# w2's block sums made by accumulating transfers, with the splits that follow them in a new order

## Chip, cores, metric

One core of one Trainium2 chip. The metric is the device time of one execution in microseconds (us). The engines are called PE (TensorE, matmuls), DVE (VectorE), ACT (ScalarE), POOL (GpSimd) and SP (SyncE, which issues DMA transfers). Each runs its own instructions in order and waits for the others by semaphores.

## What is computed

```python
xn = layernorm(x)                                 # x: 2048 x 576
q, k, v = split(xn @ wqkv)                        # 32 heads of 18
phi = lambda t: where(t > 0, t + 1, exp(t)) + 1e-6
kv = einsum("hsd,hse->hde", phi(k), v); z = phi(k).sum(over s)
s = ((phi(q) @ kv) / (phi(q) . z + 1e-6)) @ wo    # linear attention
h = gelu_tanh(xn @ w1 + b1)                       # 2048 x 4608
g = silu(h @ w2 + b2)                             # 2048 x 576
out = x + s * g
```

All is float32 at float32 precision.

## The kernel before

**Operands.** PE multiplies in a reduced form (fp32r). Each factor is therefore split in two: a rounded copy (hi, a cast on ACT) and the remainder (lo, a subtraction on DVE), and a product is hi x hi, hi x lo and lo x hi. Most products are also done by a two-by-two Strassen-Winograd scheme: seven products of block sums in place of eight of blocks. So the sums of a weight's blocks must be made and split before PE can use them.

**w2's blocks.** w2 has nine chunks of four row tiles. A chunk's blocks B(r, n) are two row tiles by half the columns (288). Four sums are needed of each: 5, 6, 4 and 7, by the numbers of the products that use them. POOL makes them with `tensor_tensor`: 5 and 6 of all chunks (and 4 of the first) early, beside the attention part, by `w2_sum`; `w2_hi` (ACT) and `w2_lo` (DVE, tile w2o) split them and SP stores them in HBM, from where the chunk steps load them. The sums 7 and 4 of the later chunks are made within the chunk steps by `sum7` and `sum4` (one and two instructions on POOL).

**The stages in time.**

- Keys: up to 163 us. Eight pairs of row tiles; a pair p has 14 steps (`at_step`). In them PE projects keys and values and sums the state kv; ACT and DVE normalise, transpose and split the next pairs' x, and do phi.
- Rounds of queries, 163 to about 283 us. A round r has 14 steps as well: PE projects two tiles of queries (products 1, 6, 7, 5, 2, 4, 3, tiles a, b, z, e) and multiplies the round before by the folded kw. POOL multiplies queries by z (`den_mul`) and divides them (`den_div`).
- Chunk steps, about 283 us to the end. Eighteen steps of 28 places each: nine chunks for one half of the rows, then nine for the other. A step makes h by two groups of seven products (`Up`), splits h and its sums, and adds seven down products (tile pm) into macc. In the first half it also makes the sums of w1 and w2 for the next chunk. The second half loads what the first has stored.

**The order** is written out by hand: `add(step, fn, ...)` puts a call in a list, `at_step` runs the list after the matmuls of that step, and `in_order` keeps every engine to the order of the calls. So an instruction that waits holds all later ones of its engine. SP's transfers are in such an order too.

**Names.** `wkq` is the weight of keys, later of queries; `split_sums(j)` splits its block sums. `xSL`, `xSH` are the splits of x's block sums. `split_kw(k)` splits row tile k of kw, after a transfer that shifts its rows (kr). `SUMS[j]` lists w2's early sums by (chunk, sum).

Of the kernel before, what the change touches and what calls it, by code (L numbers as in the profile page):

```python
# [8 lines left out]
F32 = mybir.dt.float32  # L9
# [6 lines left out]
P = 128  # L16
S = 2048
D = 576
# [8 lines left out]
CF = 4  # L27
# [15 lines left out]
def linear_attention_gated_ffn(ctx, tc, x, wqkv, wo, w1, b1, w2, b2, out):  # L43
# [97 lines left out]
    class Weight:  # L141
# [28 lines left out]
        def sums(self, raw, eng):  # L170
# [8 lines left out]
            for i, u, v in ((5, f1a, f0a), (6, f1b, T[5]), (7, f1b, f1a), (4, f0b, T[6])):  # L179
                eng.tensor_tensor(T[i], u, v, op=SUB)  # L180

        def split_sums(self, j, elo):
            self.put(lambda t: t[:, 3 + 2 * j : 5 + 2 * j], self.t[j], elo)

# [130 lines left out]
    def s_lo(p):  # L315
        cs = pair_cols(p)
        nc.vector.tensor_tensor(
            xSL[:, :, cs], s_raw[:, :8], xSH[:, :8, cs].bitcast(F32), op=SUB
        )
        r = xSH[64:, 8, cs]  # L320
        nc.vector.tensor_tensor(r, s_raw[64:, 8], r.bitcast(F32), op=SUB)

# [142 lines left out]
    w2raw, w2op = {}, {}  # L465

    def w2_load(c, pool, tag):
        src = w2[c].rearrange("p (a r n d) -> p a r n d", a=2, r=2, n=2)
        if tag == "wa":
            tiles = [pool.tile([P, KT * 2 * P], F32, tag=tag, name=f"w2r{c}{r}") for r in range(2)]  # L470
            parts = [t[:, : 2 * D].rearrange("p (a n d) -> p a n d", a=2, n=2) for t in tiles]
            for r in range(2):
                nc.sync.dma_start(parts[r], src[:, :, r])
        else:
            t = pool.tile([P, CF * D], F32, tag=tag, name=f"w2r{c}")
            nc.sync.dma_start(t, w2[c])
            t = t.rearrange("p (a r n d) -> p a r n d", a=2, r=2, n=2)
            parts = [t[:, :, r] for r in range(2)]
        w2raw[c] = parts

    def w2_block(c, i):

        B = lambda r, n: w2raw[c][r][:, :, n, :]
        return {
            5: (B(0, 0), B(0, 1), B(0, 0)),
            6: (B(1, 1), B(1, 1), B(0, 0)), 4: (B(1, 0), B(1, 0), B(1, 1)),
        }[i]

    def w2_sum(j):
        c, i = SUMS[j]  # L490
        dst, a, b = w2_block(c, i)
        nc.gpsimd.tensor_tensor(dst, a, b, op=SUB)

    def w2_hi(j):
        w2op[j] = w1r.tile([P, 2, 2, HD], F32R, tag="stw", name=f"w2o{j}")
        nc.scalar.copy(w2op[j][:, 0], w2_block(*SUMS[j])[0])

    def w2_lo(j):
        c, i = SUMS[j]
        t = w2op.pop(j)  # L500
        nc.vector.tensor_tensor(t[:, 1], w2_block(c, i)[0], t[:, 0].bitcast(F32), op=SUB)  # L501
        w2_dram[c, i] = d = dram.tile([P, 2, 2, HD], F32, name=f"op_{c}_{i}")
        nc.sync.dma_start(d, t.bitcast(F32))
# [93 lines left out]
    K_UP = (1, 6, 7, 5, 2, 4, 3)  # L597
    W2_FIRST = {2: (0,), 3: (1, 2), 4: (3,), 5: (4, 5), 6: (6,)}

    def plan_pair(p):  # L600
# [19 lines left out]
        if p == 1:  # L620
# [21 lines left out]
            add(base + 6, load_x, 4, 1)  # L642
            add(base + 6, wkq.split_sums, 0, DV)
        else:
# [27 lines left out]
        add(base + 8, phi_max, kb, eb)  # L672
        add(base + (11 if p == 1 else 10), phi_add, kb)
        add(base + 12, k_sum, kb)
        for n, j in enumerate(W2_FIRST.get(p, ())):
            add(base + (1, 3)[n], w2_sum, j)
            add(base + (4, 9)[n], w2_hi, j)
            add(base + (6, 12)[n], w2_lo, j)
        if p in (1, 3):
            add(base + 13, w2_load, {1: 1, 3: 2}[p], w2p, "w2r")  # L680
        if p == 4:
# [3 lines left out]
        if p == 7:  # L685
            add(base, nc.gpsimd.memset, kvz, 0.0)
            add(base + 5, lambda: wkq.split_sums(1, DV))
            add(base + 5, lambda: wkq.split_raw(cur["rq"][0], 0, DV))
            add(base + 9, lambda: wkq.split_sums(0, DV))
            add(base + 10, lambda: wkq.split_rest(cur["rq"][1], DV))  # L690
            add(base + 11, lambda: wkq.split_raw(cur["rq"][0], 1, DV))
        if p == 6:
            add(base + 9, lambda: wkq.sums(cur["rq"][0], GP))

# [51 lines left out]
    def load_w2_raw(n):  # L746
        raw = w2rp.tile([P, CF // 2, 2, 2, HD], F32, tag="w2raw", name=f"w2raw{n}")
        nc.sync.dma_start(raw.rearrange("p a b n d -> p (a b n d)"), w2[n % NC])
        return raw
# [222 lines left out]
    for r in range(NPAIR + 2):  # L972
# [186 lines left out]
    class W2:  # L1159
# [5 lines left out]
        def load_raw(self):  # L1165
            self.raw = raw = load_w2_raw(self.n) if self.n else w2_raw0[0]
            self.B = lambda r, n: raw[:, :, r, n, :]
            self.src = {1: self.B(0, 0), 2: self.B(1, 0), 3: self.B(1, 1), 7: self.B(0, 1)}

        def sum7(self):  # L1170
            nc.gpsimd.tensor_tensor(self.src[7], self.src[3], self.src[7], op=SUB)

        def sum4(self):
            tt = nc.gpsimd.tensor_tensor
            self.src[4] = self.src[2]
            tt(self.src[4], self.src[2], self.src[7], op=SUB)
            tt(self.src[4], self.src[4], self.src[1], op=SUB)

        def plain(self, f):
            self.src["p", f] = self.raw[:, f // 2, f % 2]  # L1180

# [14 lines left out]
    class HOps:  # L1196
# [11 lines left out]
        def S(self, i, pr):  # L1208
            A = lambda r, c: self.A[pr, r, c]
            tt = nc.gpsimd.tensor_tensor  # L1210
            src = self.src
            if i == 5:
                src[5, pr] = A(1, 0)
                tt(src[5, pr], A(1, 0), A(1, 1), op=ADD)  # L1214
            elif i == 6:
                src[6, pr] = A(0, 0)
                tt(src[6, pr], src[5, pr], A(0, 0), op=SUB)  # L1217
            elif i == 3:
                src[3, pr] = A(0, 1)
                tt(src[3, pr], A(0, 1), src[6, pr], op=SUB)  # L1220
# [21 lines left out]
    DST = {1: U1, 2: C11, 5: C22, 3: C12, 6: U1, 7: C22, 4: C21}  # L1242
    BIAS = {2: 0, 7: 1, 3: 1, 4: 0}

    def product(c, i, q2, hs, w, held):

        wh, wl = w
        ps = held.pop((CHAIN[i], q2)) if i in CHAIN else bank2(f"pm{i}")
        if i in CHAIN.values():
            held[i, q2] = ps  # L1250
        for q in range(2):
            cs = slice((q2 + q) * P, (q2 + q + 1) * P)
            seq = [(st, m, p) for p in range(2) for st, m in ((0, wh), (0, wl), (1, wh))]
            for n, (st, m, p) in enumerate(seq):
                nc.tensor.matmul(  # L1255
                    ps[:, q, :HD], hs[p][st][:, cs], m[:, p, :],
                    start=(n == 0 and i not in CHAIN), stop=(n == len(seq) - 1),
                    skip_group_check=True,
                )
        src, dst = ps[:, :, :HD], macc[:, q2 : q2 + 2, DST[i], :]  # L1260
        if c > 0 or i in (5, 6):
            nc.vector.tensor_tensor(dst, src, dst, op=ADD)  # L1262
        elif i in BIAS:
            h = BIAS[i]
            bb = b2b[:, None, h * HD : (h + 1) * HD].to_broadcast([P, 2, HD])
            nc.vector.tensor_tensor(dst, src, bb, op=ADD)
        else:
            nc.vector.tensor_copy(dst, src)

    def combine(s, eng, q=slice(0, QH)):  # L1270
        A = lambda s: macc[:, q, s, :]
        eng.tensor_tensor(A(s), A(s), A(U1), op=ADD)

# [146 lines left out]
    PW2 = {1: 3, 7: 4, 3: 6}  # L1420
    PW2_FIRST = {1: 3, 7: 4, 2: 5, 3: 6}
    W2_SUMS_NEXT = {5: 23, 6: 27}
# [22 lines left out]
    for step in range(n_chunks):  # L1445
# [15 lines left out]
        if half == 0 and c < NC - 1:  # L1461
# [116 lines left out]
```

## Time and profile before

| what | value |
|---|---|
| runs (us) | 1120.46, 1120.64, 1121.62; median 1120.64 |
| profiled execution | 1120.46 us, its span 1118.8 us |
| PE, DVE, ACT, POOL busy (us) | 1099.8, 834.3, 506.2, 485.2 |
| DMA | 257.16 MB, 230 GB/s in the mean, 64.3% of 16 engines' span |
| granted PE clock | 1.00 over the span |

Times in a row of the profile are microseconds from the span's start. A row of the timeline gives start, duration, engine, line, operation and tiles (out<-in), and in brackets the idle time before it with what ended it. Busy time of PE is modelled, since matmuls overlap; how far apart two matmuls start tells more than how long each is.

### The profile page before, as it was taken

To read this page: it belongs to the slowest core of one execution; us is meant where nothing else is said; L and a number is where in the kernel's file an instruction comes from. 1 tells how busy PE (TensorE), PEld (TensorE's weight loads), DVE (VectorE), ACT (ScalarE), POOL (GpSimd) and SP (SyncE) were. 2 spreads that over 40 slices of the span, in tenths; PEclk is the share of its full clock that TensorE was granted. 3 is DMA by queue.
4 is the path that set the end of the run, shared out by engine and by line. 5 is a ranking of instruction groups with operands and counts; after the bars stand their busy time and mean duration, and the time that the engine had idled before them with its cause. 6 is when DMAs were issued, how large, how long until landed. Compare 5 with 4: busy or idle time off the path is not lost.

```text
span 1118.8 us, 18673 instructions
## 1 busy us (share of the span) xinstructions
PE 1099.8 (98%) x6924; PEld 1014.6 (91%) x6924; DVE 834.3 (75%) x1250; ACT 506.2 (45%) x913; POOL 485.2 (43%) x411
## 2 busy tenths in 40 slices
PE   8999999999999999999999999999999999999997
PEld 7899998999898998989989889899898998988987
DVE  6878756777598988989889888666475574664756
ACT  6766554445545454454454544524233242242352
POOL 5654434655364645645556443324224133242340
PEclk9999999999999999999999999999999999999999
DMA  5855537774968468385583759977666666666243
GB/s 202 289 210 224 223 99 238 279 281 161 354 253 322 179 234 296 153 326 193 207 323 149 294 181 369 373 261 267 217 207 215 211 200 210 228 200 222 88 136 119
DMA packets 89098, 257.16 MB, mean 230 GB/s; under 512 B 9581, under 2 KB 20333, under 8 KB 86959
## 3 DMA queue, kind: packets, MB, share of 16 engines
q1 hardware_dynamic: 89007, 255.96, 64.3%
q8 instruction: 55, 0.90, 0.3%
q14 instruction: 36, 0.29, 0.1%
HBM read 155.03 MB, written 100.01 MB: 228 GB/s over the span
## 4 chain that ended last, share of the span: by engine, by line
PE 82%; DVE 7%; ACT 4%; issue 2%; DMA 2%; POOL 2%; SPq 0%; DVEq 0%; POOLq 0%; ACTq 0%
PE pm L1255 32%; PE e L1118 12%; PE zy L1118 10%; PE a L1118 10%; PE b L1118 4%; PE pl L404 4%; PE ps_s L866 2%; PE pd L1372 2%; PE e L349 1%; DVE w2o L501 1%; DMA kr<-kw 1%; DVE h_l L896 1%; PE z L349 1%; PE ps_kva L457 1%; PE a L349 1%
## 5 line engine op out<-in xcount | busy, mean ns | idle before, releaser
L1262 DVE TENSOR_TENSOR macc<-pm,macc 128x576 f32<-128x576 f32 x218 | 164.1, 753 | 48.0 <-PE pm L1255 46.8
L893 ACT CAST h_h<-g 128x512 fp32r<-128x512 f32 x204 | 120.0, 621 | 142.2 <-PE pm L1255 141.1
L896 DVE TENSOR_TENSOR h_l<-g,h_h 128x512 fp32r<-128x512 f32 x204 | 171.2, 839 | 0.0
L1223 POOL TENSOR_TENSOR mid<-g 128x512 f32<-128x512 f32 x34 | 44.1, 1296 | 187.1 <-ACT g L1126 187.1
L1118 PE MATMUL a<-xH,wa 128*128 128x512 f32 x360 | 117.1, 390 | 0.0
L1118 PEld LDWEIGHTS a<-xH,wa 128*128 128x128 f32 x360 | 67.6, 188 | 13.6
L1126 ACT ACTIVATE g<-b,b1c 128x512 f32<-128x512 f32 x36 | 24.8, 689 | 121.5 <-DVE b L1144 121.5
L1118 PE MATMUL e<-xSH,wb 128*128 128x512 f32 x216 | 66.8, 390 | 0.9 <-DVE b L1144 0.9
L1343 POOL TENSOR_TENSOR fin1l<-fin1h,fin1l 128x288 f32<-128x288 f32 x8 | 6.5, 808 | 122.0 <-DMA fin1l<-s_dram 30.3
L1217 POOL TENSOR_TENSOR g<-g 128x512 f32<-128x512 f32 x34 | 49.6, 1459 | 20.8 <-DVE h_l L896 19.5
L1135 ACT COPY mid<-a 128x512 f32<-128x512 f32 x36 | 21.2, 588 | 78.5 <-PE a L1118 78.3
L1118 PE MATMUL a<-xL,wa 128*128 128x512 f32 x144 | 56.2, 390 | 0.0
L1220 POOL TENSOR_TENSOR g<-g 128x512 f32<-128x512 f32 x34 | 49.9, 1468 | 13.1 <-DVE h_l L896 11.8
L1214 POOL TENSOR_TENSOR g<-g 128x512 f32<-128x512 f32 x34 | 51.2, 1507 | 2.7
L1138 DVE TENSOR_TENSOR mid<-b,mid 128x512 f32<-128x512 f32 x36 | 24.7, 685 | 35.7 <-PE b L1118 33.3
L1118 PE MATMUL b<-xSH,w 128*128 128x512 f32 x144 | 50.2, 389 | 0.0
L1118 PE MATMUL zy<-xH,w 128*128 128x512 f32 x144 | 50.2, 389 | 0.0
L1118 PE MATMUL zy<-xSH,w 128*128 128x512 f32 x144 | 50.2, 389 | 0.0
L1118 PE MATMUL e<-xSH,w 128*128 128x512 f32 x144 | 50.2, 389 | 0.0
L1118 PEld LDWEIGHTS e<-xSH,wb 128*128 128x128 f32 x216 | 40.5, 188 | 10.1 <-DVE b L1144 1.7
L896 DVE TENSOR_TENSOR h_l<-mid,h_h 128x512 fp32r<-128x512 f32 x34 | 43.1, 1268 | 6.0 <-ACT h_h L893 6.0
L1126 ACT ACTIVATE g<-e,b1c 128x512 f32<-128x512 f32 x36 | 24.8, 689 | 48.8 <-DVE e L1151 48.8
(928 smaller groups left out, 3580.7 us busy)
## 6 DMA issues: line engine op xcount, KB each, us to landing
op<-w SPq DMA_DIRECT2D x72, 256.0 KB
w<-op SPq DMA_DIRECT2D x72, 256.0 KB
w1raw<-w SPq DMA_DIRECT2D x18, 640.0 KB
w2raw<-w SPq DMA_DIRECT2D x10, 1152.0 KB
op_a<-wa SPq DMA_DIRECT2D x18, 640.0 KB
wa<-op_a SPq DMA_DIRECT2D x18, 640.0 KB
op<-w2o SPq DMA_DIRECT2D x19, 576.0 KB
w2r<-w SPq DMA_DIRECT2D x6, 1152.0 KB
```

The source lines that it names most:

```text
L349: nc.tensor.matmul(ps, st, mv, start=first and n == 0, stop=n == len(seq) - 1, skip_group_check=True,)
L404: nc.tensor.matmul(self.ps[n], st, self.wk(hl, k, n), start=(i == 0), stop=(i == n_all - 1))
L893: nc.scalar.copy(pair[0], src)
L896: eng.tensor_tensor(pair[1], src, pair[0].bitcast(F32), op=SUB)
L1118: nc.tensor.matmul(ps.rearrange("p (c j) -> p c j", c=4), st, mv, start=first and n == 0, stop=n == len(seq) - 1, skip_group_check=True,)
L1126: nc.scalar.activation(g, ps, AF.Gelu_apprx_tanh, bias=b1c[:, f : f + 1])
L1214: tt(src[5, pr], A(1, 0), A(1, 1), op=ADD)
L1217: tt(src[6, pr], src[5, pr], A(0, 0), op=SUB)
L1220: tt(src[3, pr], A(0, 1), src[6, pr], op=SUB)
L1223: tt(src[7, pr], A(0, 0), A(1, 0), op=SUB)
L1255: nc.tensor.matmul(ps[:, q, :HD], hs[p][st][:, cs], m[:, p, :], start=(n == 0 and i not in CHAIN), stop=(n == len(seq) - 1), skip_group_ch ...
L1262: nc.vector.tensor_tensor(dst, src, dst, op=ADD)
```

## The change

**Sums by transfers.** A DMA transfer issued by POOL can add to its target (`accum_op=ADD`). `w2_sum`, `sum7` and `sum4` become such transfers (`add_to`): POOL only begins them. Since they can add and not subtract, the signs of the scheme change: h's sums swap ADD and SUB, and the products 3, 5, 6 and 7 are subtracted from macc (`MINUS`). w2 lies in HBM in another block order, so that a block is one run of 576 numbers per partition. One operand of a sum comes straight from HBM, or from the block summed before. Sum 4 of a chunk step has a place of its own (tile w2t4), loaded by SP with B(0, 0), to which two transfers add.

**When.** A table (`W2_STARTS`, `W2_SPLITS`) sets pair and step at which a sum is begun and split. The fourth chunk's two sums move from the second and third rounds to pairs 6 and 7, and its load from the first round to pair 5.

**Splits reordered.** In pair 1 the two casts of wkq's sums come first and its second subtraction follows xSL; in the second round `split_kw` 2 and 3 come later; in the chunk steps hi and lo of sum 4 move behind w1's. The last rest of xSH (64 x 128) goes from DVE to POOL.

```diff
+        def sums_hi(self, j):
+            nc.scalar.copy(self.h[:, 3 + 2 * j : 5 + 2 * j], self.t[j])
+
+        def sums_lo(self, j, elo):
+            js = slice(3 + 2 * j, 5 + 2 * j)
+            elo.tensor_tensor(self.l[:, js], self.t[j], self.h[:, js].bitcast(F32), op=SUB)
...
-        nc.vector.tensor_tensor(r, s_raw[64:, 8], r.bitcast(F32), op=SUB)
+        nc.gpsimd.tensor_tensor(r, s_raw[64:, 8], r.bitcast(F32), op=SUB)
...
+    def w2_blocks(c):
+        return w2[c].rearrange("p (r n a d) -> p r n a d", r=2, n=2, a=2)
...
+        r, n = {5: (0, 0), 6: (1, 1), 4: (1, 0)}[i]
+        return w2raw[c][r][:, n]
+
+    def add_to(dst, src):
+        nc.gpsimd.dma_start(dst, src, accum_op=ADD)
 
     def w2_sum(j):
         c, i = SUMS[j]
-        dst, a, b = w2_block(c, i)
-        nc.gpsimd.tensor_tensor(dst, a, b, op=SUB)
+        add_to(w2_block(c, i), {5: w2_blocks(c)[:, 0, 1], 6: w2_block(c, 5), 4: w2_block(c, 6)}[i])
 
     def w2_hi(j):
-        w2op[j] = w1r.tile([P, 2, 2, HD], F32R, tag="stw", name=f"w2o{j}")
-        nc.scalar.copy(w2op[j][:, 0], w2_block(*SUMS[j])[0])
+        pool, tag, bufs = (t1, "w2o", 1) if j == 8 else (w1r, "stw", 2)
+        w2op[j] = pool.tile([P, 2, 2, HD], F32R, tag=tag, name=f"w2o{j}", bufs=bufs)
+        nc.scalar.copy(w2op[j][:, 0], w2_block(*SUMS[j]))
...
-    W2_FIRST = {2: (0,), 3: (1, 2), 4: (3,), 5: (4, 5), 6: (6,)}
+    W2_SPLITS = (
+        (2, 4, 6), (2, 9, 12), (3, 4, 6), (3, 9, 12), (4, 4, 6), (4, 9, 12), (5, 4, 6), (6, 7, 9), (7, 1, 3),
+    )
+    W2_STARTS = ((1, 7), (2, 2), (2, 11), (3, 2), (3, 11), (4, 2), (4, 11), (6, 0), (6, 8))
+    W2_LOADS = {1: (13, 1), 3: (7, 2), 5: (7, 3)}
...
-            add(base + 7, wkq.split_sums, 1, DV)
+            add(base + 6, wkq.sums_hi, 1)
+            add(base + 6, wkq.sums_hi, 0)
+            add(base + 6, wkq.sums_lo, 1, DV)
...
-            add(base + 6, wkq.split_sums, 0, DV)
+            add(base + 10, wkq.sums_lo, 0, DV)
...
-            add(base + 12, split_kw, 2, nc.vector)
-            add(base + NSP + 2, split_kw, 3, nc.vector)
-        if 1 <= r <= 6:
+            add(base + NSP + 2, split_kw, 2, nc.vector)
+            add(base + NSP + 4, split_kw, 3, nc.vector)
+        if 2 <= r <= 6:
             add(base, w2_load, r + 2, *((w1p, "wa") if r % 2 == 0 else (w2rp, "w2raw")))
-        if 2 <= r <= 7:
+        if r == 2:
+            add(base + 8, w2_sum, 2 * r + 5)
+        if 3 <= r <= 7:
             n = 2 * r + 3
+            add(base + 1, w2_sum, n + 1)
+            if r < 7:
+                add(base + 8, w2_sum, n + 2)
             for j in range(2):
-                add(base + ((0, 3) if r > 2 else (4, 5))[j], w2_sum, n + j)
-                add(base + (7 if r > 2 else 10) + j, w2_hi, n + j)
-                add(base + (9 if r > 2 else 11) + j, w2_lo, n + j)
+                add(base + 7 + j, w2_hi, n + j)
+                add(base + 9 + j, w2_lo, n + j)
...
+            if 0 < self.n < NC:
+                self.src[4] = fr.tile([P, CF // 2, HD], F32, tag="w2t4", name=f"w2t4_{self.n}", bufs=1)
+                nc.sync.dma_start(self.src[4], w2_blocks(self.n)[:, 0, 0])
 
         def sum7(self):
-            nc.gpsimd.tensor_tensor(self.src[7], self.src[3], self.src[7], op=SUB)
-
-        def sum4(self):
-            tt = nc.gpsimd.tensor_tensor
-            self.src[4] = self.src[2]
-            tt(self.src[4], self.src[2], self.src[7], op=SUB)
-            tt(self.src[4], self.src[4], self.src[1], op=SUB)
+            add_to(self.src[7], w2_blocks(self.n)[:, 1, 1])
+
+        def sum4(self, part):
+            add_to(self.src[4], self.src[7] if part else w2_blocks(self.n)[:, 1, 0])
...
         if c > 0 or i in (5, 6):
-            nc.vector.tensor_tensor(dst, src, dst, op=ADD)
+            if i in MINUS:
+                nc.vector.tensor_tensor(dst, dst, src, op=SUB)
+            else:
+                nc.vector.tensor_tensor(dst, src, dst, op=ADD)
...
-    PW2_FIRST = {1: 3, 7: 4, 2: 5, 3: 6}
+    PW2_FIRST = {1: 3, 2: 4, 7: 8, 3: 9}
...
-            add(base + 8, nxt.load_raw)
-            add(base + 20, nxt.sum7)
+            add(base + (8 if step else 10), nxt.load_raw)
+            add(base + (16 if step else 17), nxt.sum7)
+            add(base + (16 if step else 17), nxt.sum4, 0)
             add(base + 21, nxt.hi, 2)
             add(base + 21, nxt.lo, 2)
-            add(base + 22, nxt.sum4)
-            add(base + 24, nxt.hi, 4)
-            add(base + 25, nxt.lo, 4)
+            add(base + (21 if step else 22), nxt.sum4, 1)
+            add(base + 27, nxt.hi, 4)
+            add(base + 27, nxt.lo, 4)
```

How the order stands on the engines, before and after, at three places. First POOL in the first chunk step, from the last sums of h (g) to the first sums of w1 for the next chunk; w2raw1 is the second chunk of w2, w2t4_1 the new place of its sum 4. Before:

```order
L1217 TENSOR_TENSOR g_3760<-g_3791,g_3760 128x512
L1220 TENSOR_TENSOR g_3776<-g_3776,g_3760 128x512
L1171 TENSOR_TENSOR w2raw1_3720<-w2raw1_3720 128x2x288
L1176 TENSOR_TENSOR w2raw1_3720<-w2raw1_3720 128x2x288
L1177 TENSOR_TENSOR w2raw1_3720<-w2raw1_3720 128x2x288
L918 TENSOR_TENSOR w1t5_4000<-w1raw2_3585 128x256
```

and after:

```order
L1240 TENSOR_TENSOR g_3762<-g_3793,g_3762 128x512
L1243 TENSOR_TENSOR g_3778<-g_3762,g_3778 128x512
L497 DMA w2raw1_3745<-w2 128x576
L497 DMA w2t4_1_3747<-w2 128x576
L497 DMA w2t4_1_3747<-w2raw1_3745 128x576
L937 TENSOR_TENSOR w1t5_4000<-w1raw2_3585 128x256
```

The three sums keep their place in the row, as transfers; the third reads what the first has summed.

Second, ACT at the start of the second query round; a6 is the PSUM tile that PE writes next, kr2 and kr3 the row tiles of kw that arrive by transfer, e0 and scr_99 buffers of phi. Before:

```order
L435 ACTIVATE scr_99<-scr_99,c1_85 128x576
L768 CAST kw_h_2022<-kr2_2059 128x576
L361 COPY scr_99<-a6_2186 128x288
L841 CAST th01_2203<-ptp01_2197 128x640
L441 ACTIVATE scr_99<-scr_99,c2_86 128x576 x2
L768 CAST kw_h_2022<-kr3_2068 128x576
L373 ACTIVATE rt_111<-a6_2186,c0_84 128x288
```

and after:

```order
L442 ACTIVATE scr_99<-scr_99,c1_85 128x576
L368 COPY scr_99<-a6_2196 128x288
L860 CAST th01_2213<-ptp01_2207 128x640
L448 ACTIVATE scr_99<-scr_99,c2_86 128x576 x2
L787 CAST kw_h_2036<-kr2_2073 128x576
L380 ACTIVATE rt_111<-a6_2196,c0_84 128x288
L787 CAST kw_h_2036<-kr3_2082 128x576
```

Both casts of kw moved behind the copy of a6.

Third, DVE at the end of pair 1; wkq_l are the remainders of wkq's sums, xSL those of x's sums. Before:

```order
L157 TENSOR_TENSOR wkq_l<-wt_524,wkq_h 128x1152
L438 SCALAR_TENSOR_TENSOR k_164<-e_160,k_164 128x576
L157 TENSOR_TENSOR wkq_l<-wt_525,wkq_h 128x1152
L438 SCALAR_TENSOR_TENSOR k_165<-e_161,k_165 128x576
L317 TENSOR_TENSOR xSL<-scr,xSH 128x1024
L321 TENSOR_TENSOR xSH<-scr,xSH 64x128
```

and after:

```order
L187 TENSOR_TENSOR wkq_l<-wt_525,wkq_h 128x1152
L445 SCALAR_TENSOR_TENSOR k_164<-e_160,k_164 128x576
L445 SCALAR_TENSOR_TENSOR k_165<-e_161,k_165 128x576
L324 TENSOR_TENSOR xSL<-scr,xSH 128x1024
L247 BN_STATS st_654<-x_459 128x6
L248 BN_STATS st_654<-x_459 128x6
```

One subtraction of wkq_l moved behind xSL, and the rest of xSH is gone from DVE.

More of the change, by code (lines that the diff above doesn't have):

```diff
@@ L672, in plan_pair @@
         add(base + 8, phi_max, kb, eb)
[L673 to L680, printed above, removed]
+        add(base + (13 if p == 1 else 10), phi_add, kb)
+        add(base + (13 if p == 1 else 12), k_sum, kb)
+        for j, (q, at_hi, at_lo) in enumerate(W2_SPLITS):
+            if q == p:
+                add(base + at_hi, w2_hi, j)
+                add(base + at_lo, w2_lo, j)
+            if W2_STARTS[j][0] == p:
+                add(base + W2_STARTS[j][1], w2_sum, j)
+        if p in W2_LOADS:
+            at, c = W2_LOADS[p]
+            add(base + at, w2_load, c, w2p, "w2r")
         if p == 4:
@@ L692, in plan_pair @@
         if p == 6:
-            add(base + 9, lambda: wkq.sums(cur["rq"][0], GP))
+            add(base + 12, lambda: wkq.sums(cur["rq"][0], GP))
     for p in range(1, NPAIR):
@@ L746, in load_w2_raw @@
     def load_w2_raw(n):
-        raw = w2rp.tile([P, CF // 2, 2, 2, HD], F32, tag="w2raw", name=f"w2raw{n}")
-        nc.sync.dma_start(raw.rearrange("p a b n d -> p (a b n d)"), w2[n % NC])
+        raw = w2rp.tile([P, 2, 2, CF // 2, HD], F32, tag="w2raw", name=f"w2raw{n}")
+        nc.sync.dma_start(raw.rearrange("p r n a d -> p (r n a d)"), w2[n % NC])
         return raw
```

41 lines of the change are left out of this document (20 added, 21 removed).

## The prediction

> **What bounds the kernel now.** I read the page first, then the chain that ended last, then the timelines of single engines around each place where PE (TensorE) starts a matmul late.
>
> ```profile
> PE 1099.8 (98%) x6924; PEld 1014.6 (91%) x6924; DVE 834.3 (75%) x1250; ACT 506.2 (45%) x913; POOL 485.2 (43%) x411
> ```
>
> PE is busy for 98% of the span of 1118.8 us, and the change leaves its instructions as they are. So all that can be won are PE's late starts, and all that can be lost are new ones. The chain shows the chunk steps by the first matmul of each down product (start, us):
>
> ```profile
> 314.72 13.06 PE pm L1255 x96
> ...
> 680.52 22.39 PE pm L1255 x168
> 725.63 22.39 PE pm L1255 x168
> ```
>
> From 314.72 to 680.52 lie eight steps of the first half, 45.73 us each. The next, with the same matmuls but no sums to make for a chunk ahead, takes 45.11 us (680.52 to 725.63): 0.62 us a step less, 4.9 us over the eight. The first row also gives PE's pace, 13.06 us for 96 matmuls, 0.14 us each. Inside one such step, the timeline of three engines (start, us, engine, line; in brackets the idle time before):
>
> ```profile
> 368.48 1.89 POOL L1171 TENSOR_TENSOR w2raw<-w2raw 128x576 f32<-128x576 f32 x1
> 375.10 1.75 POOL L1176 TENSOR_TENSOR w2raw<-w2raw 128x576 f32<-128x576 f32 x1 [4.74 <-DVE w__4436 L896]
> 371.50 0.67 DVE L896 TENSOR_TENSOR h_l<-g,h_h 128x512 fp32r<-128x512 f32 x1
> 375.48 0.75 DVE L1262 TENSOR_TENSOR macc<-pm,macc 128x576 f32<-128x576 f32 x1
> 376.14 1.26 DVE L896 TENSOR_TENSOR h_l<-g,h_h 128x512 fp32r<-128x512 f32 x1
> 376.93 0.43 PE L1255 MATMUL pm<-w__4195,h_h 128*128 128x288 f32 x2
> 377.45 0.40 PE L1255 MATMUL pm<-w__4195,h_l 128*128 128x288 f32 x1
> ```
>
> The same subtraction takes 0.67 us where POOL rests and 1.26 us where POOL sums w2. The slowed one ends at 377.40, and PE's next matmul, due 0.27 us after the pair that began at 376.93, starts at 377.45: 0.25 us late. DVE's addition from PSUM (macc) beside the same POOL sum keeps to 0.75 us; what collides is reading two SBUF tiles beside a POOL instruction that reads SBUF.
>
> **The change part by part.** *A, chunk steps.* Three POOL sums a step become three transfers that POOL only begins. If making a transfer's descriptors doesn't slow DVE, the 1.26 us falls to 0.67, and the subtraction behind 368.48 gains as much. Ends: 0 and the whole 4.9 us. I take 0.5 us a step, 4.0, near the upper end: a transfer reads no tile on POOL, and the macc row says that reading is what collides; but POOL's sums of h stay and go on slowing DVE earlier in the step. What is late next is the sums of w1 (L918), which follow on POOL behind the third transfer; that one now waits for two landings. Behind them wait ACT's and DVE's splits for the next chunk. The two earlier transfers are issued by some 370.5 (368.48 and two issues of 1 us, below); the w1 sums begin now after 375.10 and two sums of about 1.75, so they come later than now only if a landing takes over 7 us. The Trainium skill (SBUF — State Buffer, Who interferes with whom) says that a DVE instruction with two SBUF inputs contends with GpSimd instructions that read SBUF, not with ones that only write; Perfetto Trace Analysis, DMA Instruction — SWDGE, adds that such a DMA instruction reads no tensor. The trace agrees as to reading (1.26 against 0.67); no row shows a POOL transfer. By these pages A is near its upper end.
>
> By the nearest row alone, any POOL work costs what a sum costs, and A is 0 (first rival).
>
> *B, second query round.*
>
> ```profile
> 181.10 0.67 ACT L768 CAST kw_h<-kr 128x576 fp32r<-128x576 f32 x1 [1.34 <-DMA kr<-kw]
> 180.98 0.29 PE L349 MATMUL e<-wkq_rl,xH 128*128 128x288 f32 x1
> 182.12 0.40 PE L349 MATMUL a<-wkq_h,xH 128*128 128x288 f32 x1 [0.86 <-ACT scr L361]
> 183.16 0.29 PE L349 MATMUL a<-wkq_rl,xH 128*128 128x288 f32 x1
> 184.38 0.40 PE L349 MATMUL z<-wkq_h,xH 128*128 128x288 f32 x1 [0.92 <-DVE scr L367]
> ```
>
> ACT stands 1.34 us before a cast that waits for a transfer; the copy of a into scr (L361), which PE waits for, stands behind it. PE loses 1.14 and 1.22 less 0.14 each: 2.1 us. The two casts (split_kw 2 and 3) go behind that copy. Their first use is the attention product after seven of the round's 14 steps; that covers them, and without it the wait would be back. I take 2.0 (ends 1.0, if DVE stays late, and 2.1).
>
> *C and D, later rounds.*
>
> ```profile
> 195.78 3.36 DVE L501 TENSOR_TENSOR w2o<-w2r,w2o 128x576 fp32r<-128x576 f32 x2 [0.80 <-issue]
> 200.17 0.29 PE L349 MATMUL a<-wkq_rl,xH 128*128 128x288 f32 x1
> 201.07 0.40 PE L349 MATMUL z<-wkq_h,xH 128*128 128x288 f32 x1 [0.61 <-DVE scr L367]
> 202.11 0.29 PE L349 MATMUL z<-wkq_rl,xH 128*128 128x288 f32 x1
> 202.65 0.40 PE L349 MATMUL e<-wkq_h,xSH 128*128 128x288 f32 x1 [0.24 <-DVE scr L357]
> 242.16 3.63 DVE L501 TENSOR_TENSOR w2o<-w2r,w2o 128x576 fp32r<-128x576 f32 x2
> 239.27 0.66 ACT L496 CAST w2o<-w2r 128x576 fp32r<-128x576 f32 x1
> 243.24 1.95 POOL L492 TENSOR_TENSOR w2r<-w2r 128x576 f32<-128x576 f32 x1
> 248.91 0.29 PE L349 MATMUL z<-wkq_rl,xH 128*128 128x288 f32 x1
> 249.31 0.40 PE L349 MATMUL e<-wkq_h,xSH 128*128 128x288 f32 x1
> ```
>
> C: the fourth chunk's two splits (195.78) leave this round, and with them PE's late starts, 0.90 and 0.54 less 0.14 each: 1.2 us. They go beside the keys, below. D: in the four rounds after it the pair of splits takes 3.63 us beside POOL's sum; with the sum gone I take two of about 1 us, between 0.67 and 1.26. PE starts 0.26 us late (248.91 to 249.31); in four rounds that is 1.0, and I take it whole (ends 0 and 1.0).
>
> *E, keys.*
>
> ```profile
> 47.14 1.34 DVE L157 TENSOR_TENSOR wkq_l<-wt,wkq_h 128x1152 fp32r<-128x1152 f32 x1
> 49.47 0.29 PE L349 MATMUL b<-wkq_l,xSH 128*128 128x288 f32 x1
> 50.34 0.40 PE L349 MATMUL b<-wkq_h,xSL 128*128 128x288 f32 x1 [0.58 <-DVE xSL L317]
> 61.46 0.68 ACT L496 CAST w2o<-w2r 128x576 fp32r<-128x576 f32 x1 [3.81 <-POOL w2r L492]
> 68.22 0.29 PE L349 MATMUL b<-wkq_l,xSH 128*128 128x288 f32 x1
> 68.94 0.40 PE L349 MATMUL b<-wkq_h,xSL 128*128 128x288 f32 x1 [0.43 <-DVE xSL L317]
> ```
>
> The second half of the weight split (47.14) goes behind xSL: xSL comes 1.34 us sooner, and PE's 0.73 us of waiting goes. The later wait, 0.58 us, follows an ACT that stood 3.81 us for POOL's first w2 sum, which queued behind POOL's sums of z. The first transfer is begun eleven steps ahead, before those sums. I take 1.2 of 1.3 (lower end 0).
>
> *What is added.* Bounds for the transfers (chain; groups; PE's waits; windows, whose columns are the busy times of PE, PEld, DVE, ACT and POOL, then clock, DMA share, GB/s):
>
> ```profile
> 111.90 3.74 PE pl L404 x28
> ...
> 129.14 7.45 PE pl L404 x56
> ...
> 199.89 7.58 DMA w2r<-w
> L248 POOL TENSOR_TENSOR mv<-mv 128x1 f32<-128x1 f32 x14 | 2.7, 195 | 1.1
> PE e L1118 <- DVE b L1144: 0.9, 2, 0.7
> 129.00:146.00 17.00, 17.00 (x133) 16.82 (x132) 11.07 (x15) 8.18 (x13) 10.38 (x7) 1.00 0.65 238
> 212.00:227.50 15.50, 15.40 (x118) 15.17 (x117) 11.62 (x20) 7.66 (x17) 8.44 (x7) 1.00 0.82 289
> 680.00:725.60 45.60, 45.60 (x273) 41.60 (x271) 31.93 (x43) 21.99 (x32) 14.93 (x10) 1.00 1.02 393
> ```
>
> POOL's part of one: between its smallest instruction, 0.20 us, and the sum it replaces, 1.9; I take 1 us, which POOL has. The landing: a load of four times the bytes took 7.58 us, a quarter of that is 1.9 us, both as estimates for an addition of unknown price. A pair lasts 17.24 us in 14 steps, so seven steps are 8.6 us: ACT, which waits in order for a landing with the phi functions behind it, finds it done even at 7.58. A round lasts 15.6 us (202.11 to 248.91 are three). In it POOL begins the second transfer where the sum at 243.24 stood, and ACT's cast of it stands a round after 239.27, 11.6 us on. The Trainium skill (DMA: Bandwidth & Descriptors, Anatomy of one DMA) gives 2.0 us plus the bytes at 436 GB/s, by estimate 2.7 us here; it says nothing of an addition, and no run here shows one yet. By it ACT never waits and the 1.0 us allowed below falls away, 1111.1 us.
>
> Bytes: two transfers of 0.29 MB a round, up to three times that if the target is read and written, add 38 to 114 GB/s to 289; 393 is the most a row shows. I allow 1.0 us for waits of this kind, between -0.7 (PE's longest wait for b, at the first chunk, whose splits are reordered too and which I count at nothing) and the second rival's price.
>
> At nothing: the reversed signs (same operations, operands and sizes), the new block order in memory (same bytes), the third sum's own place and its load (SP issues it at a time when it has room), xSH's small rest on POOL (used a pair's steps later), and the fourth chunk's splits beside pairs 6 and 7, where DVE is busy 11.07 of 17.00 us; without that room they would cost C again.
>
> Sum: 4.0 + 2.0 + 1.2 + 1.0 + 1.2 - 1.0 = 8.4 us. The profiled execution took 1120.46 us (its span and 1.7 around it), the lowest of the three, whose median is 1120.64; so 1112.1 us.
>
> **The rivals.** *First: making descriptors slows DVE as a sum does.* For it: the row 1.26 against 0.67 is all that shows POOL beside DVE. Then A and D are 0 and 3.4 us is left: 1117.1. Against it: macc's 0.75.
>
> *Second, slower: the additions land late.* An adding transfer may hold the DMA engines several times as long as its bytes, in rounds whose DMA share is 0.82. ACT then waits at each of the eight splits begun seven steps ahead beside the keys. The 3.81 us that ACT stood cost PE 0.58, so ACT has about 3.2 us to spare, and loss begins at a landing of 8.6 + 3.2 = 11.8 us. A landing of twice 7.58, 15.2 us, loses 3.4 x 8 = 27 us; D and E go too, and A, B and C keep 7.2: 1140. The sign turns near 12.7 us, where eight waits eat the 7.2. Against it: 7.58 was for four times the bytes. The Trainium skill (SBUF — State Buffer, SBUF: two separate sides) has a rule against this change: DVE in a two-port mode keeps GpSimd from writing descriptors, and a transfer of 0.62 us then took 3.1 us. The same page gives tensor_tensor, most of DVE's work here, no such mode; no run shown so far has a transfer begun by POOL.
>
> *Third: the change doesn't do what it says.* POOL's transfers wait in order for the loads they add to, and h, den and w1 sums behind them come late; each stall returns elsewhere. For it: in the rounds a chunk's load now has eight steps, 8.9 us, against 7.58 in the row. Against it: den and h sums have several us to spare behind POOL. The sum is then within 1 us of 0: 1120.
>
> **How the numbers follow.** The forecast has 0.6, the first rival 0.18, the second 0.14, the third 0.08. The lower end, 1108.5, is A to E at their upper ends (10.5) and the 0.7, 1109.3, with 0.8 more for late starts of the same kind too small to be priced here; the upper, 1121.0, takes in the first and third. A measurement of this kernel can tell 0.2%, 2.2 us, from no change. So faster 0.78, same 0.08, slower 0.14.
>
> **What would show it.** Right: first-half steps of about 45.2 us, h_l beside POOL's transfers at 0.67, no late PE start at the second round's a and z, ACT idle little before w2o. Wrong: ACT waiting for DMAs in w2o, h_l still at 1.26, or the steps at 45.7.

## The result, and the profile after

The changed kernel takes 1120.46 us (median of 14 runs, 1117.67 to 1123.53), the kernel before, on the same chips, 1120.76 (14 runs, 1120.05 to 1124.73): ratio 0.9995, 95% interval 0.9984 to 1.0005. No difference can be told, where 1112.1 was forecast. The profiled execution took 1122.14 us, its span is 1120.4 us.

The first page of the profile (busy time of each engine) and the chain that ended last, with PE's runs of down products (start, us):

```profile
PE 1098.9 (98%) x6924; PEld 1017.2 (91%) x6924; DVE 810.8 (72%) x1242; ACT 505.4 (45%) x913; POOL 459.5 (41%) x419
```

```profile
359.13 12.88 PE pm L1279 x96
376.43 6.00 PE pm L1279 x43
...
635.98 12.89 PE pm L1279 x96
```

POOL has 25.7 us less to do and DVE 23.5, as the change intends. But the six steps from 359.13 to 635.98 take 46.14 us each, where they took 45.73: a first-half step is longer than before, not shorter.

To see where that comes from, PE's late starts are summed by stage: the distance between the starts of neighbouring matmuls, less the median distance of their line, wherever that is over 25 ns (matmuls at a slow clock are in it). The last column is the best kernel of the experiments below, e8; the edges are the same for all three. Each column is of one profiled execution; that of the changed kernel lies 1.7 us above its median.

| stage (us) | before | after | e8 |
|---|---|---|---|
| 0–20, start | 5.2 | 5.1 | 5.4 |
| 20–79, first keys | 5.2 | 3.8 | 3.9 |
| 79–163, later keys | 1.3 | 1.1 | 1.3 |
| 163–196, first rounds | 4.8 | 5.6 | 2.6 |
| 196–296, later rounds | 4.4 | 5.4 | 1.6 |
| 296–704, first-half steps | 6.1 | 7.3 | 0.6 |
| 704 to the end | 1.3 | 1.3 | 1.3 |
| sum | 28.2 | 29.5 | 16.6 |

The sums differ by 1.3 us, the spans by 1.6. Only the keys gained. Three places lost.

**First place: chunk steps.** The timelines of POOL, DVE and PE in the step that was shown of before (start, us; in brackets the idle time before):

```profile
367.15 0.89 POOL L497 DMA_DIRECT2D w2raw<-w  x1
367.74 1.19 POOL L497 DMA_DIRECT2D w2t<-w  x1
374.19 0.86 POOL L497 DMA_DIRECT2D w2t<-w2raw  x1 [5.25 <-DMA w2t<-w]
374.75 1.07 POOL L937 TENSOR_TENSOR w1t<-w1raw 128x256 f32<-128x256 f32 x1
368.35 0.68 DVE L915 TENSOR_TENSOR h_l<-g,h_h 128x512 fp32r<-128x512 f32 x1
374.64 1.73 DVE L915 TENSOR_TENSOR h_l<-g,h_h 128x512 fp32r<-128x512 f32 x1
375.44 0.43 PE L1279 MATMUL pm<-w__4197,h_h 128*128 128x288 f32 x2
376.43 0.40 PE L1279 MATMUL pm<-w__4197,h_l 128*128 128x288 f32 x1 [0.57 <-DVE h_l L915]
```

Beside a transfer that POOL begins (367.74) h_l takes 0.68 us, as hoped. But POOL's part of the third transfer is done at 375.05, and POOL goes straight on with the sums of w1 (L937; the two records overlap by 0.30 us). Before, the first of these sums stood 3.90 us later:

```profile
378.65 1.19 POOL L918 TENSOR_TENSOR w1t<-w1raw 128x256 f32<-128x256 f32 x1
```

Against product 3's pair of matmuls (375.44 here, 376.93 before) it now comes 2.4 us earlier. It meets the h_l that product 3 waits for. That h_l ends at 376.37, 0.55 us behind the end of the w1 sum at 375.82, and alone it takes 0.68: nearly all of it came after the sum. PE starts 0.99 us after the pair ahead of it, where 0.27 was due: 0.73 us late, against 0.25 before.

**Second place: the second round.** ACT, POOL, DVE and PE:

```profile
180.63 0.67 ACT L787 CAST kw_h<-kr 128x576 fp32r<-128x576 f32 x1 [0.25 <-DMA kr<-kw]
181.18 1.41 POOL L823 TENSOR_TENSOR scr<-scr,zb 128x576 f32<-128x576 f32 x1
181.33 1.87 DVE L788 TENSOR_TENSOR kw_l<-kr,kw_h 128x576 fp32r<-128x576 f32 x1 [0.62 <-ACT kw_h L787]
183.13 0.45 DVE L364 SCALAR_TENSOR_TENSOR rt<-e,scr 128x288 f32<-128x288 f32 x1
183.50 0.74 DVE L788 TENSOR_TENSOR kw_l<-kr,kw_h 128x576 fp32r<-128x576 f32 x1
183.63 0.40 PE L356 MATMUL e<-wkq_h,xSH 128*128 128x288 f32 x1 [1.53 <-DVE rt L364]
```

ACT's cast no longer stands ahead of what PE needs, but its second half does: the subtraction kw_l waits for the cast, then lies behind POOL's multiplication (it ends 0.61 us after that, and alone takes 0.74), and rt, which PE waits for, stands behind it on DVE. The two start nearly together, POOL 0.15 us ahead. In e1 and e5 below, whose order is the same here, DVE starts first, by 0.05 and 0.03 us; kw_l then takes 0.76 us, and PE is only 0.4 us late at e. So this loss is not in every execution: of the seven profiled ones with this order, POOL came first in five.

**Third place: the rounds.** SP's issue of a chunk's load, then POOL, ACT, DVE and PE:

```profile
216.32 1.99 SPq L483 DMA_DIRECT2D w2r<-w  x2
225.22 0.88 POOL L497 DMA_DIRECT2D w2r<-w  x1 [7.11 <-DMA w2r<-w]
225.83 1.75 POOL L823 TENSOR_TENSOR e<-rt,zb 128x576 f32<-128x576 f32 x1
233.15 0.88 POOL L497 DMA_DIRECT2D w2r<-w2r  x1 [4.18 <-DMA w2r<-w]
233.76 2.58 POOL L836 TENSOR_TENSOR pbuf<-rt,den 128x576 f32<-128x576 f32 x2
235.26 0.25 ACT L845 COPY pbuf<-pbuf 128x64 f32<-128x64 f32 x1 [4.86 <-POOL pbuf L836]
241.90 0.29 DVE L865 TENSOR_TENSOR th<-ptp,th 64x128 fp32r<-64x128 f32 x1
242.34 1.30 PE L853 MATMUL ptp<-ident,pbuf 128*128 128x128 f32 x5 [2.35 <-DVE th L865]
```

POOL waits 7.11 us for a chunk's load, and den_mul (L823) waits behind it; then 4.18 us for the first addition's landing, and den_div (L836) waits behind that. ACT, with den_div's result as its next work, stands 4.86 us. What is queued behind it comes late, among it the cast of th (L860, at 240.46); DVE's th follows that cast, and PE, which waits for DVE's th, is 2.51 us late.

Behind the second and the third place there is a further loss. Windows (busy times of PE, PEld, DVE, ACT, POOL; granted clock, DMA share, GB/s):

```profile
183.70:187.00 3.30, 3.30 (x15) 3.30 (x16) 3.16 (x8) 0.12 (x1) 1.17 (x1) 0.53 0.66 270
242.40:245.30 2.90, 2.90 (x13) 2.90 (x14) 2.21 (x2) 0.21 (x2) 1.80 (x2) 0.50 0.97 349
```

For about 3 us after each gap PE runs at half its clock: 0.47 x 3.30 and 0.50 x 2.90 make another 1.55 and 1.45 us.

### The profile page after: what moved, and what is told of

The parts are those of the page before. It is cut to its first block, busy times and chain, and to the rows that moved or that the text cites. A ratio compares the mean times of both kernels' runs of the same rounds, so it can differ in the third digit from the quotient of the medians.

```text
span 1120.4 us, 18755 instructions
## 1 busy us (share of the span) xinstructions
PE 1098.9 (98%) x6924; PEld 1017.2 (91%) x6924; DVE 810.8 (72%) x1242; ACT 505.4 (45%) x913; POOL 459.5 (41%) x419
## 4 chain that ended last, share of the span: by engine, by line
PE 90%; DVE 4%; ACT 3%; DMA 1%; issue 1%; POOL 1%; DVEq 0%; POOLq 0%; ACTq 0%
PE pm L1279 32%; PE e L1141 12%; PE a L1141 10%; PE zy L1141 10%; PE ps_s L885 5%; PE pl L411 5%; PE b L1141 4%; PE e L356 2%; PE z L356 2%; PE a L356 2%; PE pd L1402 2%; DVE h_l L915 1%; PE ps_kva L464 1%; DMA kr<-kw 1%; PE b L356 1%
## 5 line engine op out<-in xcount | busy, mean ns | idle before, releaser
L1287 DVE TENSOR_TENSOR macc<-macc,pm 128x576 f32<-128x576 f32 x128 | 96.1, 751 | 36.8 <-PE pm L1279 36.7
L1289 DVE TENSOR_TENSOR macc<-pm,macc 128x576 f32<-128x576 f32 x90 | 68.0, 755 | 18.4 <-PE pm L1279 17.6
L1243 POOL TENSOR_TENSOR g<-g 128x512 f32<-128x512 f32 x34 | 49.9, 1467 | 13.1 <-DVE h_l L915 11.8
```

The costliest lines, as they stand in the source:

```text
L1243: tt(src[3, pr], src[6, pr], A(0, 1), op=SUB)
L1287: nc.vector.tensor_tensor(dst, dst, src, op=SUB)
```

## The experiments

All are the changed kernel with the edits shown, and their times stand against the kernel before, run beside them on the same chip.

**e1, w1's sums between the second and the third transfer.**

```diff
-        T={5: 24, 6: 24, 7: 25, 4: 25},
+        T={5: 18, 6: 18, 7: 18, 4: 18},
```

> First theory (w1's sums): in the changed kernel POOL's sums of w1 start right behind the third transfer and run beside the subtraction h_l of product 3, which takes 1.73 us and makes PE 0.73 to 0.98 us late in seven steps, 6.0 us together. Here these sums stand between the second and the third transfer, beside earlier h_l that have some time to spare: the late starts at product 3 fall under 0.1 us, some 0.2 us a step come back earlier, time 1115 to 1116. Rival (the transfer): the third transfer itself, or what it moves, slows that h_l, and it still stands beside it: late starts of 0.7 to 1.0 us stay, time 1120.

1119.68 us, ratio 0.9991 (0.9981 to 1.0002). POOL and DVE in the step:

```profile
374.98 0.88 POOL L497 DMA_DIRECT2D w2t<-w2raw  x1 [0.98 <-DMA w2t<-w]
372.14 1.26 DVE L915 TENSOR_TENSOR h_l<-g,h_h 128x512 fp32r<-128x512 f32 x1
374.65 0.68 DVE L915 TENSOR_TENSOR h_l<-g,h_h 128x512 fp32r<-128x512 f32 x1
```

The third transfer stands beside an h_l of 0.68 us: it is not what slows it. But the w1 sums, now earlier, slow two earlier h_l (one is shown at 372.14) and DVE is late all the same: the late starts of the stage fall to 4.9 us, not to the 1 or 2 that the expected time needs. The cause stands, the place was no better. The time fell by less still, since in this run's profiled execution the rounds, which the edit leaves alone, lost 8.0 us and not 5.4 (see e3).

**e5, DVE's order instead.** The split of product 3's h, hi and lo, goes one place ahead (in both tables of `PH`), and w2's remainder behind all h_l; POOL keeps its order.

```diff
-            add(base + 21, nxt.lo, 2)
+            add(base + 24, nxt.lo, 2)
...
-            (4, 1): 17, (5, 1): 18, (5, 0): 19, (6, 0): 20, (3, 0): 21, (3, 1): 22, (6, 1): 23,
+            (4, 1): 17, (5, 1): 18, (5, 0): 19, (6, 0): 20, (3, 0): 21, (3, 1): 21, (6, 1): 23,
```

> In the chunk steps DVE takes the h_l that product 3 needs one place earlier, and the remainder of w2's block 2 (0.75 us) goes behind all h_l; POOL is as in the changed kernel. Theory (w1's sums hold h_l): h_l is done about 0.7 us before the first w1 sum starts and takes 0.68 us; the late starts of 0.73 to 0.98 us at product 3 go, those between 296 and 704 us fall from 7.3 to 1 to 2 us, time 1114 to 1115. Rival (DVE's time is what lacks): the next h_l, beside the w1 sums at 1.25 us, comes late in its turn, 0.5 us a step stay, time 1118.

1115.91 us, ratio 0.9958 (0.9946 to 0.9970). The chain:

```profile
360.01 22.47 PE pm L1279 x168
...
631.12 22.47 PE pm L1279 x168
```

Steps of 45.19 us (271.11 for six), whole runs of 168 matmuls, late starts of 0.6 us in the stage. This is the gain that was forecast for A, and the transfers gave it only with DVE's order.

**e4 and e10, the chunk steps' sums on POOL again**, e4 in the changed order, e10 with the order of e5 (and e3's first line, and e7's sums).

```diff
-            add_to(self.src[7], w2_blocks(self.n)[:, 1, 1])
+            nc.gpsimd.tensor_tensor(self.src[7], self.src[7], self.src[3], op=ADD)
...
-            add_to(self.src[4], self.src[7] if part else w2_blocks(self.n)[:, 1, 0])
+            nc.gpsimd.tensor_tensor(self.src[4], self.src[4], self.src[7 if part else 2], op=ADD)
```

> The chunk steps' three sums as POOL additions again, at the places of the changed kernel (with the place of sum 4 and its load), all else as changed. First theory (w1's sums): w1's sums follow even sooner, the late starts at product 3 stay at 0.6 to 1.0 us, and h_l beside the w2 sums is at 1.26 us again for another 0.2 us a step: 1121 to 1122. Rival (the transfer slows DVE): late starts at product 3 back at 0.25 us, time 1116.

> As e9, with the chunk steps' sums too as POOL additions (place of sum 4 and order of DVE kept): only the sums beside the keys are transfers. Theory (the order of DVE and the transfers are both needed): POOL's w2 sums and w1 sums stand in one block of some 10 us beside all the late h_l at 1.25 us; late starts of 0.4 to 0.9 us a step, 1114 to 1118. Rival (the order alone does it): within 1 us of e9.

e4 1132.04 us, ratio 1.0099 (1.0085 to 1.0113), which neither theory had; e10 1123.38 us, 1.0027 (1.0017 to 1.0037), 12.8 us above e9, and outside what I gave it too. In e10, POOL, DVE and PE:

```profile
365.94 3.76 POOL L1200 TENSOR_TENSOR w2t<-w2t,w2raw 128x576 f32<-128x576 f32 x2
369.65 1.21 POOL L941 TENSOR_TENSOR w1t<-w1raw 128x256 f32<-128x256 f32 x1
368.98 1.27 DVE L919 TENSOR_TENSOR h_l<-g,h_h 128x512 fp32r<-128x512 f32 x1
373.47 0.51 PE L1279 MATMUL pm<-w__4197,h_h 128*128 128x288 f32 x2 [1.16 <-DVE macc L1287]
```

With no landing to wait for, POOL works through all sums in one block, every late h_l is slow, and DVE as a whole falls behind: PE is 1.3 us late at product 3 in each step. So against sums in one block the transfers are worth much more than the 0.62 us a step that I could read from before, where the sums stood in pieces with a pause between. DVE's order of e5 with POOL's sums in such pieces was not run; how much of A that order alone would win stays open.

**e2 and e7, the rounds.** e2 puts den_mul ahead of the first addition, the second behind den_div, and its split later; e7 makes these sums on POOL again, at the places of before (0 and 3 of the round behind the load). The diff is e2's.

```diff
-        if r == 2:
-            add(base + 8, w2_sum, 2 * r + 5)
+        if 2 <= r <= 6:
+            add(base + 12, w2_sum, 2 * r + 5)
...
-            add(base + 1, w2_sum, n + 1)
-            if r < 7:
-                add(base + 8, w2_sum, n + 2)
+            add(base + 4, w2_sum, n + 1)
             for j in range(2):
-                add(base + 7 + j, w2_hi, n + j)
-                add(base + 9 + j, w2_lo, n + j)
+                add(base + (7, 12)[j], w2_hi, n + j)
+                add(base + (9, 12)[j], w2_lo, n + j)
```

> Theory (POOL waits in order): in the rounds POOL stands 7.1 us for a load and 4.2 us for a landing, with den_mul and den_div behind it, and PE loses 2.51 us at one place and then runs at half its clock for 3 us. Here den_mul goes ahead of the first transfer, the second stands behind den_div, and the second split comes later: the 2.51 us and the halved clock go, PE's late starts between 196 and 296 us fall from 5.4 to about 2 us, time 1115.5 to 1117. Rival (the traffic): the added bytes make loads and landings late for everybody; ACT or DVE then waits for w2r instead, time 1119 to 1121.

> The rounds' sums (chunks 4 to 8) as POOL additions again, at the places of the kernel before; keys and chunk steps as changed. Theory (POOL waits in order for landings): POOL's waits of 7.1 and 4.2 us go, with them the 2.51 us at 240 us and the slow clock behind it; D's late starts of 0.26 us in four rounds come back: 1116.5 to 1117.5, with less scatter. Rival (bytes or places other than POOL's waits): 1120.

e2 1114.35 us, ratio 0.9935 (0.9922 to 0.9949); e7 1114.63 us, 0.9944 (0.9931 to 0.9957). POOL's waits for loads and landings in w2r (us in total, times, longest), of the changed kernel, of e2 and of e7:

```profile
POOL w2r L497 <- DMA w2r<-w: 22.1, 8, 7.1
```

```profile
POOL w2r L497 <- DMA w2r<-w: 6.0, 4, 2.9
```

```profile
POOL w2r L497 <- DMA w2r<-w: 1.1, 1, 1.1
```

e7's one wait is beside the keys; in its rounds POOL begins no transfer.

Either way the 2.51 us and the slow clock behind it are gone, and the late starts of 196 to 296 us fall from 5.4 to 1.3 (e2) and 2.9 (e7). POOL's in-order waits were the cause; the transfers as such do no harm in the rounds. Both gained more than expected: some 3 us more come from the chunk steps, where in four of eight steps (one in the changed kernel) h_l now happened to start early enough (see the last section). That part is luck.

**e3, e6 and e8: the splits of kw, and all together.** e3 moves both splits one place later; e6 is e2, e3 and e5 together; e8 is e6 with the second split where the change had it (4).

```diff
-            add(base + NSP + 2, split_kw, 2, nc.vector)
-            add(base + NSP + 4, split_kw, 3, nc.vector)
+            add(base + NSP + 3, split_kw, 2, nc.vector)
+            add(base + NSP + 5, split_kw, 3, nc.vector)
```

> Theory (one subtraction in the way): kw_l of row tile 2 waits on DVE for kr's landing with PE's rt<-e behind it; PE is 1.69 us late and then at half clock for 3.4 us, another 1.5 us. Here both splits of kw go one step later, behind rt<-e: both go, time 1117 to 1117.5. Rival (the landing): ACT's cast still waits for kr ahead of rt<-a, so the wait moves to a or z, 1 us late there: time 1119.5.

> The order of e5 in the chunk steps, the places of e2 in the rounds and those of e3 for the splits of kw, together. Theory (three separate causes): e2's 1114.35, less its chunk steps' late starts of 4.4 us to 1, less 1.69 us at the second round's e and half of the 1.5 us of slow clock behind it: 1108 to 1110, and less scatter than the changed kernel. Rival (one late place only makes room for the next): 1112 to 1114.

> As e6, but the second split of kw stays at the changed kernel's place (behind rt<-e and the first, ahead of den). Theory: the 0.84 us that PE waited for kw_l at the second attention product in e3 and e6 goes, nothing else moves: 1109.5 to 1110. Rival: rt<-z behind it on DVE is late for e by as much: 1110.6.

e3 1120.89 us, ratio 1.0002 (0.9986 to 1.0019). DVE and PE in it:

```profile
182.65 0.46 DVE L364 SCALAR_TENSOR_TENSOR rt<-e,scr 128x288 f32<-128x288 f32 x1
186.52 1.73 DVE L788 TENSOR_TENSOR kw_l<-kr,kw_h 128x576 fp32r<-128x576 f32 x1
188.30 0.53 PE L885 MATMUL ps_s<-kw_l,th 128*128 128x288 f32 x2 [0.68 <-DVE kw_l L788]
```

The 1.69 us at e went, 0.84 us came at kw_l's first use, and the rounds behind, untouched there, lost what was left (7.9 us of late starts where the changed kernel had 5.4). This is not e3's doing: e1, e4 and e5, whose rounds are untouched too, lost 8.0, 9.3 and 8.2 us there. PE's gap at the third place was 2.84 us in e3 and 2.94 to 3.54 in those three, and 2.35 in the profiled execution of the changed kernel, which is thus the mildest of the five. Neither side of the expectation held. e6 1110.59 us, ratio 0.9914 (0.9900 to 0.9928), 0.6 above the range of its theory: its 0.84 us is e3's. e8, without it, 1109.38 us, ratio 0.9901 (0.9888 to 0.9915): 11.1 us faster than before and the best of all, with late starts of 16.6 us. In the table the first rounds, the later rounds and the chunk steps have 3.0, 3.8 and 6.7 us less of late starts than in the changed kernel: each of the three causes is gone. They are not quite independent, since e2's and e7's edits in the rounds freed some chunk steps as well.

**e9, e8 with the rounds' sums on POOL** (e7's edit).

> As e8, with the rounds' sums as POOL additions at the places of the kernel before (as in e7). Theory (D: a POOL sum slows DVE's splits there): about 1 us slower than e8, 1110.5 to 1111.5. Rival (with nothing to wait for, POOL sums are as good in the rounds): equal to e8 or up to 1 us faster, and less scatter.

1110.63 us, ratio 0.9920 (0.9908 to 0.9933), 1.25 above e8. By these medians D's price of 1.0 us was about right, once the waits are out of the way.

**e11, gaps made on purpose.** The order of e5, and ahead of product 3's h_l, in chunk steps 1 to 7, one more needless DVE operation from step to step.

```diff
+            def hold_vector(n):
+                for _ in range(n):
+                    nc.vector.tensor_tensor(u2_sb, u2_sb, u2_sb, op=ALU.max)
+            if 1 <= step <= 7:
+                add(base + 21, hold_vector, 1 + step)
```

> The order of e5, with two to eight needless DVE operations of 0.68 us (a maximum of a tile with itself) ahead of product 3's h_l in chunk steps 1 to 7, so that PE stands about 0.7, 1.4, 2.1, 2.7, 3.4, 4.1 and 4.8 us there. Theory (a gap long enough halves the granted clock for the 3.4 us behind it): full clock behind the gaps of up to 1.4 us, 0.5 behind those from 2.7 us, and 2.1 us either way. Rival (the slow clock behind 1.69 and 2.51 us came from something else in the rounds, such as the transfers): clock 1.0 behind all seven gaps.

1168.13 us in its one run. PE behind the first two gaps, and the windows that follow them:

```profile
380.42 0.50 PE L1279 MATMUL pm<-w__4197,h_h 128*128 128x288 f32 x2 [1.92 <-DVE macc L1287]
429.02 0.82 PE L1279 MATMUL pm<-w__4701,h_h 128*128 128x288 f32 x2 [3.19 <-DVE macc L1287]
```

```profile
380.60:383.60 3.00, 3.00 (x24) 3.00 (x24) 2.84 (x4) 2.04 (x6) 0.98 (x2) 1.00 0.53 197
429.30:434.60 5.30, 5.30 (x23) 5.30 (x23) 2.26 (x4) 1.54 (x4) 0.19 (x1) 0.50 0.15 61
```

The gaps came out longer than planned. Behind 1.92 us the clock is full; behind 3.19 us and the five longer ones it is 0.50 or 0.51, over windows of 2.6 to 5.3 us. POOL begins the step's third transfer some 3 to 4 us ahead of the end of the first gap (377.44) as of the second (424.90), so the transfer does not tell them apart, and in four of the six slow windows the DMA share is 0.02 or less: the gap itself slows the clock.

## Why the prediction was wrong, point by point

By the table, the chunk steps lost 1.2 us where 4.0 was to be won, and the rounds lost 1.8 where 4.2, less the 1.0 allowed, was to be won; the first keys won 1.4 against 1.2 forecast.

- **A, 4.0 us: right in its mechanism, wrong in its sentence on what is late next.** h_l beside a transfer takes 0.68 us, the rival that descriptors slow DVE is out, and e5 shows 0.54 us a step, 4.3 for eight, where I took 0.5. The failing step is "What is late next is the sums of w1": I asked only whether they come later than at 378.6. They came 3.9 us earlier, 2.4 of them against PE's work in the step, and beside the one h_l with no time to spare. The row that prices that, 1.26 us beside a POOL sum, I had quoted myself; it was 1.73.
- **B, 2.0 us: ACT's half of the split was followed, DVE's was not.** The late starts at a and z fell to 0.2 us and below; kw_l of the same split, still ahead of rt, made 1.69 us and the slow clock 1.55. My bound for "if DVE stays late" was a gain of 1.0; in this execution it was a loss of 1.1. Where kw_l starts ahead of POOL's multiplication (e1, e5), 0.4 us at e is all that is lost.
- **C and D, 2.2 us: gained, and lost again by a term that I had allowed at 1.0.** Their late starts are gone, but POOL's waits cost 2.51 and 1.45 us in this execution; in e1, e3, e4 and e5, whose later rounds have the same places, the stage lost 7.9 to 9.3 us in place of 5.4. That is the third rival's mechanism, to which I gave 0.08. I set a load of 7.58 us against eight steps of 8.9, and a landing against what waits for the sum. In the trace the load was ready 8.9 us after SP began it (216.32 to 225.22), so there was nothing to spare, and what counted was den_mul and den_div behind it in POOL's order. "Several us to spare" was not priced by a row.
- **E, 1.2 us: right.** 5.2 to 3.8 us, 1.4.
- **The second rival is out.** Over all additions, from begin to landing:

```profile
DMA to landing us min/median/max: 3.5/5.9/9.6
```

The longest lies under the 11.8 us from which it loses, and ACT waits only 1.7 us in all for the splits w2o, in two waits. The median is about twice what I worked out from the Trainium skill (DMA: Bandwidth & Descriptors, Anatomy of one DMA), 2.7 us, so the measurement decides against that estimate for an adding transfer.

Taken together: 8.4 us were there, and e8 got 11.1 with the same transfers. By the table, e8 won 5.5 us in the chunk steps against 4.0 forecast, 5.0 in the rounds against 4.2, and 1.4 in the first keys against 1.2. So the time was there to be won; the order around the transfers took it back. Since e8 has reorderings that the change lacks, it does not show that each single price was right.

## To carry to other kernels

When work leaves an engine that runs in order, ask of the next item on it not only whether it comes too late but whom it meets if it comes early. A transfer that adds costs its engine 0.9 to 1.2 us, but its wait for a load or a landing holds all that is queued behind it; put it behind the instructions that others wait for. A moved step is followed on every engine it uses, and a wait of PE of 1.5 us or more is priced with a chance of half a clock for some 3 us behind it.

## What the hardware showed that was not expected

**DVE and POOL take turns by whole instructions.** In e7, two steps, POOL's first w1 sum and DVE's h_l:

```profile
554.17 1.09 POOL L941 TENSOR_TENSOR w1t<-w1raw 128x256 f32<-128x256 f32 x1
553.74 0.68 DVE L919 TENSOR_TENSOR h_l<-g,h_h 128x512 fp32r<-128x512 f32 x1
...
645.54 1.09 POOL L941 TENSOR_TENSOR w1t<-w1raw 128x256 f32<-128x256 f32 x1
645.15 2.03 DVE L919 TENSOR_TENSOR h_l<-g,h_h 128x512 fp32r<-128x512 f32 x1
```

An h_l that starts 0.43 us ahead of the w1 sum is untouched, one that starts 0.39 us ahead ends 0.55 us after that sum. In these rows POOL's sum stands right behind a transfer that POOL begins. The second round's kw_l meets a POOL instruction that stands behind another computation; in e5:

```profile
182.01 0.76 DVE L788 TENSOR_TENSOR kw_l<-kr,kw_h 128x576 fp32r<-128x576 f32 x1 [0.44 <-ACT kw_h L787]
182.03 2.02 POOL L823 TENSOR_TENSOR scr<-scr,zb 128x576 f32<-128x576 f32 x1
```

Here DVE starts first and keeps its 0.76 us, and POOL takes 2.02 us where it takes 1.41 when it is first; in e4 POOL starts first, at 181.65, and kw_l, at 181.67, takes 2.00 us. The Trainium skill (SBUF — State Buffer, SBUF: two separate sides) says that whichever starts first gets the shared ports for the whole instruction and the other fully blocks. The trace agrees that the one blocks for the other's whole length, and for kw_l also on who goes first; with h_l, behind a transfer, the one with the earlier recorded start lost. Why stays open.

**A gap of PE halves its clock, but not each time.** In all these traces a slow stretch lasts 3.41 us or twice that (but for the last, at the program's end), and two of one trace start a multiple of 3.41 us apart, such as 183.90 and 241.92 in the changed kernel (17 times 3.413). So the clock changes on a grid, and a gap can lie within one stretch of it or across two. The same wait for rt, 1.53 us idle in the changed kernel and 1.54 in e2, lies in one stretch each time. The stretch of the changed kernel, then that of e2:

```profile
180.48:183.90 3.42, 1.84 (x12) 1.37 (x12) 2.80 (x4) 1.63 (x3) 2.11 (x2) 1.00 0.77 267
```

```profile
182.62:186.03 3.41, 1.87 (x14) 1.64 (x13) 3.34 (x6) 0.46 (x1) 0.83 (x1) 1.00 0.99 393
```

PE is busy for 1.84 and 1.87 us in them; the next stretch has half a clock in the changed kernel, and the full clock in e2. The longer gap in e3, behind the late ptp of the rounds, lies across two stretches:

```profile
245.52 0.74 PE L853 MATMUL ptp<-ident,pbuf 128*128 128x128 f32 x5 [2.84 <-DVE th L865]
```

```profile
240.47:243.89 3.42, 2.21 (x17) 1.97 (x15) 0.00 (x0) 1.42 (x4) 0.93 (x2) 1.00 0.25 49
243.89:247.30 3.41, 1.78 (x15) 1.81 (x16) 2.89 (x4) 1.92 (x5) 2.76 (x2) 1.00 0.84 169
```

Behind it the clock stays full. So 1.53 and 2.35 us of idleness (changed kernel) were followed by half a clock, 1.54, 1.92 and 2.84 us (e2, e11, e3) were not, and 3.19 us and more (e11) always were. Over all traces of this case, from 20 us on, a full-clock stretch of the grid in which PE was busy for 1.53 us or less was always followed by half a clock, one with 1.9 us or more never, and between them (1.65 to 1.88) both came. The Trainium skill (TensorE: Matmul & The Clock Gate, Part 1: The HAM clock gate) tells of a window of 3.4 us that runs freely, whatever the kernel does. The trace agrees, with its grid of 3.41 us; the page names an idle window as what slows the clock, and here a stretch in which PE was busy for half of the time was enough. I take it that this and the close start of kw_l and POOL are much of why the changed kernel's runs scatter over 5.9 us; no run shows that.
